# Attention and expert layer on one core: the turning of x moved ahead of the exponentials, logits by unit, first loads on two queues

## Chip, cores and metric

The kernel runs on one core of a Trainium2 chip. The metric is the time of one execution on the device in microseconds (us). Before the change it is 720.43 us, the median of three runs (719.71 to 723.58).

The core has a matrix engine (PE, with its weight loads PEld), a vector engine (DVE), an activation engine (ACT), a general engine (POOL) and a queue engine (SP) that here only issues transfers. ACT and POOL can issue transfers too. Matrix results go to eight PSUM banks of 128 x 512 numbers.

## What is computed

Sliding-window causal attention over 8 batches of 8 heads (576 positions, 64 numbers a head, a window of 64), then a layer with 8 experts, of which each token takes the one with the largest logit.

```python
scores = scale * q @ k.transpose(0, 1, 3, 2)
mask = (rel >= 0) & (rel < 64)
attn = softmax(where(mask, scores, -1e9))
x = (attn @ v).transpose(0, 2, 1, 3).reshape(4608, 512)

logits = x @ w_gate                      # 4608 x 8
e = argmax(logits, axis=1)
gate = softmax(logits)[row, e]
out[row] = gate[row] * (relu(x[row] @ w1[e]) @ w2[e])   # 512 -> 1024 -> 512
```

All is in float32.

## The kernel before, in words

The work has two stages. The first is an attention loop of 48 steps (up to about 220 us), the second runs the experts over tiles of 256 sorted tokens. The change touches the first stage and its seam with the second.

**Units and steps.** A *unit* is a pair of batches (`bg`, four of them) and a pair of heads (`g`, four). A unit has 1152 tokens, nine blocks of 128, and is done in three steps of three blocks, so there are 16 units and N = 48 steps. `step(s)` (line 941) works on several steps at once, as a pipeline written out by hand. Every engine runs its instructions in the order in which the program issues them. In one call of `step(s)` that order is:

- `scored(s + 1)` (628): PE, queries by keys into banks 0 and 1. `masked` (641): DVE adds the mask and takes the largest. `softened` (651): ACT, six exponentials.
- `weighted(s - 1)` (674): PE, values by turned probabilities into bank 6.
- `logit(s - 3)` (711): PE, the turned x of a step by the gate weights into bank 7.
- `flipped(s)` (659, 661): PE turns the probabilities, DVE copies the result of head 0 to `pT0`, ACT that of head 1 to `pT1`.
- `divided(s - 1)` (684 to 688): DVE divides by the sums of the exponentials and writes x to `xs`.
- loads for later units (every third step), all on SP: `load_rests`, `load_v`, `load_qk`. `load_v` also makes two copies of v on POOL.
- `turned(s + 3)` (595, 587): PE turns q and k, ACT copies. Steps 0 and 1 of a unit turn eight blocks, step 2 turns two.
- `x_turned(s - 2)` (699, 702): PE turns x, ACT copies it to `xT`.
- what stands in `todo[s]`: the routing of a finished pair of batches (`choose`, `place`, `weigh`, `store`), weight loads on ACT's queue, sums of weights on POOL.

Results of PE that ACT or DVE copies out go to banks 2 to 5 in turn (`tr_ring`): two from `flipped`, two or one from `turned`, one from `x_turned`.

**Ready logits.** In the last unit of a pair of batches `logit` returns true (`ripe`), and `by_tokens` copies that step's logits to `lgT`, turns them and writes them to `logits` by token. After the third such step `after` puts the routing into `todo`.

**The first table.** In the last routing inside the loop, `first_tiles` (902) runs in step 45: DVE makes a table of matches `hi_e`, PE multiplies it 54 times (914), DVE makes `perm_e` of the result, and POOL gathers the first tile of expert 0's tokens (`gather_first`, 280).

**Ahead of the loop** (920 to 928) SP issues 40 transfers: q and k of unit 0, gate weights, a zero row, the rests of the first pair (positions 512 to 575 of q, k, v), v of unit 0, q and k of unit 1, v of unit 1, q and k of unit 2. A transfer of q, k or v brings 128 KB in runs of 256 bytes.

**After the loop** (984 to 1044) the last `weighted`, the last logits and their routing run between parts of the first expert tile: `turn` turns the gathered tokens, `hidden` and `output` are its products, whose results use banks 0, 1, 6 and 4, 5, 7.

`any_number` (1092) is a branch for token counts that don't occur with these inputs.

Of the kernel before, what the change touches and what calls it, by code (L numbers as in the profile page):

```python
# [11 lines left out]
F32 = mybir.dt.float32  # L12
# [3 lines left out]
ALU = mybir.AluOpType  # L16
AX = mybir.AxisListType
# [19 lines left out]
def kernel(  # L37
# [458 lines left out]
    with tc.manual_schedule(), ExitStack() as held, ExitStack() as brief:  # L496
# [2 lines left out]
        rp = held.enter_context(tc.tile_pool(name="rp", bufs=2))  # L499
        att = brief.enter_context(tc.tile_pool(name="att", bufs=2))  # L500
        xp = brief.enter_context(tc.tile_pool(name="xp", bufs=3))
        sc_ring, tr_ring = cycle((0, 1)), cycle((2, 3, 4, 5))


# [32 lines left out]
        def load_qk(u):  # L537
            bg, g = units[u]
            qks[u] = [qk_m(((u % 3 + 2) % 3 * 2 + n) * 1024, BG, NV, 2, D) for n in range(2)]
            for i in range(BG):  # L540
                for t, src in zip(qks[u], (q, k)):
                    for h in range(2):
                        nc.sync.dma_start(
                            out=t[:, i, :, h, :],
                            in_=src[bg * BG + i, 2 * g + h, 0:SM, :].rearrange("(p j) d -> p j d", j=NV),
                        )

        def load_rests(bg):

            at = 6144 + bg % 2 * 2048  # L550
            vr = qk_m(at + 1024, BG, H, D)
            rests[bg] = [qk_m(at, H, D), qk_m(at + 512, H, D), vr]
            for t, src in zip(rests[bg], (q, k)):
                for i in range(BG):
                    nc.sync.dma_start(
                        out=t[i * D : (i + 1) * D], in_=src[bg * BG + i, :, SM:S, :].rearrange("h p d -> p h d")
                    )
            for i in range(BG):
                nc.sync.dma_start(out=vr[D:P, i], in_=v[bg * BG + i, :, SM:S, :].rearrange("h p d -> p h d"))
# [87 lines left out]
        def softened(prs, mx):  # L647
            for h in range(2):
                for m in range(ST):
                    y = prs[h][:, m, :]  # L650
                    nc.scalar.activation(out=y, in_=y, func=AF.Exp, scale=-1.0, bias=mx[:, h, m : m + 1])  # L651
            return prs
# [12 lines left out]
        def weighted(s, pTs):  # L665
            u, c = divmod(s, NST)
            bg, g = units[u]
            va, vb = v_ring[u % NVR]
            px = banks[6](0, 2, ST, VW)
            for m in range(ST):  # L670
                for a, (bp, i) in enumerate(blocks_of(c * ST + m)):
                    vt = va[:, bp, i // 2] if i % 2 or i == 0 else vb[:, bp, i // 2 - 1]
                    for h in range(2):
                        nc.tensor.matmul(  # L674
                            px[a * D : (a + 1) * D, h, m, :], lhsT=pTs[h][:, m, a * D : (a + 1) * D],
                            rhs=vt[:, h, :], start=True, stop=True, skip_group_check=True,
                        )
            return px
# [35 lines left out]
                )  # L714
            return g == NG - 1

        def by_tokens(bg, c):

            if c == 0:
                logits_of[bg] = rp.tile([P, NTB, E], F32, name="logits")  # L720
            lgT = rp.tile([ST * GE, P], F32, name="lgT")
            nc.scalar.copy(out=lgT[:], in_=lgs[bg][:, c, :])
            yield
            tr = banks[next(tr_ring)](0, ST, P)
            nc.tensor.transpose(out=tr[:, 0, 0 : ST * GE], in_=lgT[:], identity=ident[0 : ST * GE, 0 : ST * GE])
            V.tensor_copy(
                out=logits_of[bg][:, c * ST : (c + 1) * ST, :],
                in_=tr[:, 0, 0 : ST * GE].rearrange("p (m e) -> p m e", e=GE)[:, :, 0:E],
            )

        last = B // BG - 1
# [146 lines left out]
        def after(s, routing, bg):  # L878

            do = lambda n, op: todo.setdefault(s + n, []).append(op)  # L880
            part = lambda: next(routing, None)
            if bg < last - 1:
                for n in range(5):
                    do(n, part)

                for m in range(NTB):
                    do(5 + m * 2 // 3, partial(place, bg * NTB + m))
                    do(5 + m * 2 // 3, partial(weigh, bg, m, G))
                    if m % ST == ST - 1:
                        do(5 + m * 2 // 3, partial(store, bg, m // ST, G))  # L890
                return

            for n in (0, 0, 1, 2, 2):
                do(n, part)
            for m in range(NTB):
                do(3 + m // 3, partial(place, bg * NTB + m))
                do((2, 2, 3, 3, 4, 4, 4, 5, 5)[m], partial(weigh, bg, m, nc.scalar if m in (2, 6) else G))
                if m % ST == ST - 1:
                    do(3 + m // ST, partial(store, bg, m // ST, G))
            do(6, first_tiles)  # L900

        def first_tiles():

            V.scalar_tensor_tensor(
                out=key[:], in0=rkhi[:, 0:NJE], scalar=1.0, in1=oh_all[:, 0, 0:NJE], op0=ALU.add, op1=ALU.mult
            )
            V.tensor_tensor(
                out=hi_e[:], in0=_inner(key[:], NE * C), in1=_ins(hi_id[:, C + 1 : C + 1 + NE * C], 1, NJE),
                op=ALU.is_equal,
            )  # L910
            slots = banks[next(tr_ring)](0, NE * C)
            for j in range(NJE):
                for i in range(2):
                    nc.tensor.matmul(
                        slots, lhsT=lo[:, i, j], rhs=hi_e[:, j], start=(i + j == 0), stop=(i + j == NJE)
                    )
            V.tensor_scalar(out=perm_e[:], in0=slots, scalar1=-1.0, scalar2=float(NT), op0=ALU.mult, op1=ALU.add)
            gather_first(perm_e[:, 0:C])

        N = NU * NST  # L920
        load_qk(0)
        nc.sync.dma_start(out=wg[:, :, 0:E], in_=moe_w_gate.rearrange("(g p) e -> p g e", p=P))
        nc.sync.dma_start(out=x_dram[NT : NT + 1, :], in_=zrow[:])
        load_rests(0)
        load_v(0)
        load_qk(1)
        load_v(1)
        load_qk(2)

        for g in range(NG):  # L930
            step = NST * (g // 2) + g % 2 + 1
# [122 lines left out]
    with tc.manual_schedule():  # L1054
# [36 lines left out]

        def any_number():

            tiles_of = rt.tile([P, E, NTILE], F32, name="tiles_of")
            V.tensor_tensor(
                out=tiles_of[:], in0=_inner(cum[:], NTILE), in1=_ins(lane[:, 0:NTILE], 1, E), op=ALU.is_le
            )
            with nc.allow_low_precision("integers"):
                V.tensor_reduce(out=expert_i[:], in_=tiles_of[:].rearrange("p e t -> p t e"), axis=AX.X, op=ALU.add)
# [60 lines left out]
```

## Time and profile before

| what | us |
|---|---|
| median of three runs | 720.43 (719.71 to 723.58) |
| the profiled execution, its time | 726.15 |
| the profiled execution, its span (first to last instruction) | 724.4 |
| first `weighted` starts | 22.02 |
| `weighted` of step 2 to that of step 45 | 177.67 |
| `weighted` of step 45 to the last | 15.40 |
| from there to 240 us (first expert tile, last routing), PE busy throughout | 21.11 |
| mean granted PE clock over the span | 0.989 |

The span is what the trace shows; the time of the same execution is 1.75 us longer. In a line of the timeline the columns are start, busy time, engine, line of the program, operation, what is written and read, shape and count; in brackets stands how long the engine stood idle before and what ended that. PE's instructions overlap, so the busy time of a group is longer than the distance to the start of the next group. "PEclk" and the third column from the right in a table of stretches are the clock granted to PE, 1.00 being full speed. The DMA share can exceed 1, since transfers overlap within an engine.

### The profile page before, as it was taken

The page shows a single profiled execution, that of the slowest core. Times are in us where ns is not written, and L with a number is a line of the kernel's source. Part 1 is how long each engine was busy: PE and PEld are TensorE (multiplying, and loading weights), DVE is VectorE, ACT ScalarE, POOL GpSimd, SP SyncE. Part 2 cuts the span into 40 slices and gives each one's busy share as a digit, 9 for nine tenths or more (in the row PEclk, how much of TensorE's full clock was granted, in tenths as well). Part 3 has the DMA queues.
Part 4 walks back from the last instruction along what each step waited for, and adds up shares of the span by engine and source line. Part 5 has one row for each costly group of instructions (what it writes and reads, how often), then busy time and mean ns, then how long its engine had stood idle before and what let it go on. Part 6 is the DMA issues. An engine that isn't in the chain of part 4 may idle for free. (4 is left out here: it accounts for less than half of the span.)

```text
span 724.4 us, 17946 instructions
## 1 busy us (share of the span) xinstructions
PE 689.7 (95%) x6882; PEld 607.1 (84%) x6882; DVE 497.8 (69%) x1636; ACT 258.5 (36%) x653; POOL 350.7 (48%) x360
## 2 busy tenths in 40 slices
PE   5999999999879999999999999999999999999993
PEld 3887788888768898797999999899889799889993
DVE  3575898898965858675866686677766677666731
ACT  4787788888754211111211221112111111111110
POOL 4213748459375025937462356445274745272011
PEclk9999999999999999999999999999999999999997
DMA  8998898789361382715211531440261620111000
GB/s 159 219 195 186 176 188 230 168 188 235 106 194 47 121 291 81 258 59 202 102 38 60 161 133 57 154 170 30 88 243 59 242 69 30 61 37 61 2 30 28
DMA packets 137289, 93.37 MB, mean 129 GB/s; under 512 B 117009, under 2 KB 117009, under 8 KB 137171
## 3 DMA queue, kind: packets, MB, share of 16 engines
q1 hardware_dynamic: 127858, 62.16, 32.5%
q0 software_dynamic: 8736, 27.53, 11.7%
q10 hardware_dynamic: 576, 2.10, 0.9%
q8 instruction: 74, 1.21, 0.7%
q14 instruction: 45, 0.36, 0.2%
HBM read 72.89 MB, written 20.45 MB: 129 GB/s over the span
## 5 line engine op out<-in xcount | busy, mean ns | idle before, releaser
L315 DVE STREAM_TRANSPOSE v_m<-qk_m 32x256 f32<-32x256 f32 x304 | 132.4, 435 | 9.0 <-DMA qk_m<-x_dram,at_g 3.4
L344 PE MATMUL bank<-qk_m,s 128*128 128x128 f32 x1024 | 122.5, 275 | 1.0 <-DVE qk_m L365 1.0
L344 PEld LDWEIGHTS bank<-qk_m,s 128*128 128x128 f32 x1024 | 118.3, 192 | 1.2 <-issue 1.2
L275 POOL DMA_INDIRECT qk_m<-x_dram,at_g x38 | 41.0, 1080 | 142.4 <-DVE v_m L315 114.0
L651 ACT ACTIVATE pr<-pr,mx 128x128 f32<-128x128 f32 x288 | 89.7, 391 | 36.3 <-DVE mx L641 36.3
L344 PE MATMUL bank<-qk_m,w 128*128 128x128 f32 x768 | 93.8, 275 | 1.0 <-PEq L1077 0.9
L344 PEld LDWEIGHTS bank<-qk_m,w 128*128 128x128 f32 x768 | 90.6, 192 | 4.6 <-issue 4.2
L641 DVE CUSTOM_DVE_ANT_0 pr<-bank,mask 128x128 f32<-128x128 f32 x288 | 64.4, 286 | 30.7 <-PE bank L628 28.1
L295 POOL DMA_INDIRECT out_dram<-v_m,at_s x42 | 42.5, 1012 | 87.7 <-DVE v_m L384 85.1
L384 DVE TENSOR_TENSOR v_m<-bank,v_m 128x256 f32<-128x256 f32 (+1 forms) x95 | 43.8, 480 | 45.0 <-PE bank L388 30.1
L569 POOL COPY v_m<-v_m 64x520 f32<-64x520 f32 x32 | 19.8, 619 | 73.1 <-DMA v_m<-in_v_dram 72.5
L140 POOL TENSOR_TENSOR s<-w 128x1024 f32<-128x1024 f32 x22 | 52.2, 2372 | 0.0
L674 PEld LDWEIGHTS bank<-v_m,pT 128*64 128x64 f32 x1152 | 41.3, 141 | 12.0 <-DVE xs L688 5.8
L674 PE MATMUL bank<-v_m,pT 128*64 128x65 f32 x1152 | 47.9, 232 | 2.9 <-DVE xs L688 2.8
L388 PE MATMUL bank<-qkT_m,v_m 128*128 128x256 f32 x216 | 48.3, 379 | 0.0
L351 ACT COPY qk_m<-bank 128x512 f32<-128x512 f32 x16 | 9.4, 587 | 108.8 <-PE bank L344 63.2
L628 PE MATMUL bank<-qkT_m 64*64 64x128 f32 x1152 | 45.9, 290 | 0.1
L388 PEld LDWEIGHTS bank<-qkT_m,v_m 128*128 128x128 f32 x216 | 41.0, 190 | 5.5
L595 PE MATMUL bank<-ident,qk_m 128*128 128x128 f32 x256 | 37.0, 288 | 8.9 <-DMA qk_m<-in_q_dram 7.7
L444 PEld LDWEIGHTS bank<-qk_m,w 128*128 128x128 f32 x320 | 43.9, 190 | 0.9 <-issue 0.7
L444 PE MATMUL bank<-qk_m,w 128*128 128x160 f32 x320 | 44.4, 299 | 0.4 <-ACT qk_m L327 0.4
L659 PE MATMUL bank<-ident,pr 128*128 128x128 f32 x288 | 43.1, 287 | 0.0
(174 smaller groups left out, 1231.1 us busy)
## 6 DMA issues: line engine op xcount, KB each, us to landing
w<-in_moe_w_dram SPq DMA_DIRECT2D x11, 2048.0 KB, 10.0
qk_m<-in_q_dram SPq DMA_DIRECT2D x72, 128.0 KB, 3.8
qk_m<-in_k_dram SPq DMA_DIRECT2D x72, 128.0 KB, 3.7
v_m<-in_v_dram SPq DMA_DIRECT2D x64, 128.0 KB, 3.9
qk_m<-in_moe_w_dram SPq DMA_DIRECT2D x3, 2048.0 KB, 10.4
x_dram<-xs POOLq DMA_DIRECT2D x6, 512.0 KB
x_dram<-xs POOLq DMA_DIRECT2D x3, 768.0 KB
w<-in_moe_w_dram ACTq DMA_DIRECT2D x4, 512.0 KB, 4.3
```

The lines of the kernel that those rows point to most:

```text
L140: op()
L295: put = G.indirect_dma_start(out=out[:, :], out_offset=bass.IndirectOffsetOnAxis(ap=at_s[:, c : c + 1], axis=0), in_=ys[c], in_offset=None ...
L315: V.transpose(out=xn[b * QD : (b + 1) * QD, :, :, a * QD : (a + 1) * QD].rearrange("p c g i -> p (c g) i"), in_=rows[a * QD : (a + 1) * QD ...
L344: nc.tensor.matmul(acc[:, f, :], lhsT=a[:, g, f * P : (f + 1) * P], rhs=b[:, g, :], start=(first and f == 0 and g == 0), stop=(g == HG - 1 ...
L384: plus = lambda out, a, b: V.tensor_tensor(out=out, in0=a, in1=b, op=ALU.add)
L388: nc.tensor.matmul(acc, lhsT=a[:, f, :], rhs=b[:, f, :], start=(start and f == 0), stop=(stop and f == HF - 1), skip_group_check=True,)
L444: nc.tensor.matmul(acc[:, i], lhsT=w1[:, g, f * P : (f + 1) * P], rhs=xq[:, g].rearrange("p c s -> p (c s)")[:, 0:HALF], start=(i + g == 0 ...
L628: nc.tensor.matmul(out_, lhsT=qT[rows, t, a * WINDOW : (a + 1) * WINDOW], rhs=rhs, start=True, stop=True, skip_group_check=True,)
L641: V.tensor_tensor_reduce(out=prs[h][:, m, :], in0=scs[h][:, m, :], in1=mask[:, m0 + m, :], scale=-scale, scalar=-2 * MASKED, op0=ALU.add, ...
L651: nc.scalar.activation(out=y, in_=y, func=AF.Exp, scale=-1.0, bias=mx[:, h, m : m + 1])
L659: nc.tensor.transpose(out=tr[:, m, :], in_=prs[h][:, m, :], identity=ident[:])
L674: nc.tensor.matmul(px[a * D : (a + 1) * D, h, m, :], lhsT=pTs[h][:, m, a * D : (a + 1) * D], rhs=vt[:, h, :], start=True, stop=True, skip_ ...
```

## The change

- Ahead of the loop, the k transfers of unit 0 (four) and of the first rests (two) are issued on ACT's queue. The order becomes: q and k of unit 0, first rests, q and k of unit 1, v of units 0 and 1, gate weights, q and k of unit 2, the zero row.
- In `step(s)`, `x_turned(s - 2)` moves from behind `turned(s + 3)` to a place behind `logit` and ahead of the exponentials of step s + 1 and of `flipped(s)`. `masked` and `softened` are called separately for it.
- `logit` runs only in steps with s mod 3 = 2, then for three steps at once; `by_tokens` then copies, turns and writes all three at once, with a tile of its own pool.
- `first_tiles` is split: its DVE part stays in step 45, its products and the gather go to step 46.
- `weighted` of the last two steps writes to banks 0 and 1 in place of 6.
- `any_number` has its table in other memory.

```diff
@@ load_qk, load_rests
-                for t, src in zip(qks[u], (q, k)):
+                for t, src, queue in zip(qks[u], (q, k), (nc.sync, nc.sync if u else nc.scalar)):
                     for h in range(2):
-                        nc.sync.dma_start(
+                        queue.dma_start(
...
-            for t, src in zip(rests[bg], (q, k)):
+            for t, src, queue in zip(rests[bg], (q, k), (nc.sync, nc.sync if bg else nc.scalar)):
                 for i in range(BG):
-                    nc.sync.dma_start(
+                    queue.dma_start(
@@ weighted
-            px = banks[6](0, 2, ST, VW)
+            px = banks[6 if s < N - 2 else s - N + 2](0, 2, ST, VW)
@@ by_tokens
-        def by_tokens(bg, c):
+        def by_tokens(bg, c, n=1):
...
-            lgT = rp.tile([ST * GE, P], F32, name="lgT")
-            nc.scalar.copy(out=lgT[:], in_=lgs[bg][:, c, :])
+            lgT = (rp if n == 1 else lt).tile([ST * GE, n, P], F32, name=f"lgT{n}")
+            nc.scalar.copy(out=lgT[:], in_=lgs[bg][:, c : c + n, :])
             yield
-            tr = banks[next(tr_ring)](0, ST, P)
-            nc.tensor.transpose(out=tr[:, 0, 0 : ST * GE], in_=lgT[:], identity=ident[0 : ST * GE, 0 : ST * GE])
+            tr = banks[next(tr_ring)](0, n, ST * GE)
+            for i in range(n):
+                nc.tensor.transpose(out=tr[:, i], in_=lgT[:, i], identity=ident[0 : ST * GE, 0 : ST * GE])
...
@@ after
-            do(6, first_tiles)
+            table = first_tiles()
+            do(6, partial(next, table))
+            do(7, partial(next, table))
@@ first_tiles
                 op=ALU.is_equal,
             )
+            yield
             slots = banks[next(tr_ring)](0, NE * C)
...
             gather_first(perm_e[:, 0:C])
+            yield
@@ ahead of the loop
         load_qk(0)
+        load_rests(0)
+        load_qk(1)
+        load_v(0)
+        load_v(1)
         nc.sync.dma_start(out=wg[:, :, 0:E], in_=moe_w_gate.rearrange("(g p) e -> p g e", p=P))
+        load_qk(2)
         nc.sync.dma_start(out=x_dram[NT : NT + 1, :], in_=zrow[:])
-        load_rests(0)
-        load_v(0)
-        load_qk(1)
-        load_v(1)
-        load_qk(2)
@@ step
             if 0 <= s + 1 < N:
-                prs[s + 1] = softened(*masked(s + 1, scored(s + 1)))
+                prs[s + 1] = masked(s + 1, scored(s + 1))
             if 0 <= s - 1 < N:
                 px = weighted(s - 1, pTs.pop(s - 1))
-            ripe = 0 <= s - 3 < N and logit(s - 3)
+            ripe = 0 <= s - 3 < N and s % NST == NST - 1 and [logit(n) for n in range(s - 5, s - 2)][-1]
+            if 0 <= s - 2 < N:
+                x_turned(s - 2)
+            if 0 <= s + 1 < N:
+                prs[s + 1] = softened(*prs[s + 1])
             if 0 <= s < N:
                 pTs[s] = flipped(prs.pop(s))
...
             if s + 3 < N:
                 turned(s + 3)
-            if 0 <= s - 2 < N:
-                x_turned(s - 2)
             for op in todo.pop(s, ()):
                 op()
             if ripe:
-                bg, c = (s - 3) // (NG * NST), (s - 3) % NST
-                parts = by_tokens(bg, c)
+                bg = (s - 3) // (NG * NST)
+                parts = by_tokens(bg, 0, NST)
                 next(parts)
                 todo.setdefault(s + 1, []).append(partial(next, parts, None))
-                if c == NST - 1:
-                    after(s + 1, choose(bg), bg)
+                after(s + 1, choose(bg), bg)
```

More of the change, by code (lines that the diff above doesn't have):

```diff
@@ L501 @@
         xp = brief.enter_context(tc.tile_pool(name="xp", bufs=3))
+        lt = brief.enter_context(tc.tile_pool(name="lt", bufs=1))
         sc_ring, tr_ring = cycle((0, 1)), cycle((2, 3, 4, 5))
@@ L715, in logit @@
             return g == NG - 1
-        def by_tokens(bg, c):
+        def by_tokens(bg, c, n=1):
             if c == 0:
                 logits_of[bg] = rp.tile([P, NTB, E], F32, name="logits")
-            lgT = rp.tile([ST * GE, P], F32, name="lgT")
-            nc.scalar.copy(out=lgT[:], in_=lgs[bg][:, c, :])
+            lgT = (rp if n == 1 else lt).tile([ST * GE, n, P], F32, name=f"lgT{n}")
+            nc.scalar.copy(out=lgT[:], in_=lgs[bg][:, c : c + n, :])
             yield
-            tr = banks[next(tr_ring)](0, ST, P)
-            nc.tensor.transpose(out=tr[:, 0, 0 : ST * GE], in_=lgT[:], identity=ident[0 : ST * GE, 0 : ST * GE])
+            tr = banks[next(tr_ring)](0, n, ST * GE)
+            for i in range(n):
+                nc.tensor.transpose(out=tr[:, i], in_=lgT[:, i], identity=ident[0 : ST * GE, 0 : ST * GE])
             V.tensor_copy(
-                out=logits_of[bg][:, c * ST : (c + 1) * ST, :],
-                in_=tr[:, 0, 0 : ST * GE].rearrange("p (m e) -> p m e", e=GE)[:, :, 0:E],
+                out=logits_of[bg][:, c * ST : (c + n) * ST, :],
+                in_=tr.rearrange("p n me -> p (n me)").rearrange("p (m e) -> p m e", e=GE)[:, :, 0:E],
             )
@@ L1092, in any_number @@
         def any_number():
-            tiles_of = rt.tile([P, E, NTILE], F32, name="tiles_of")
+            tiles_of = v_m(2080, E, NTILE)
             V.tensor_tensor(
-                out=tiles_of[:], in0=_inner(cum[:], NTILE), in1=_ins(lane[:, 0:NTILE], 1, E), op=ALU.is_le
+                out=tiles_of, in0=_inner(cum[:], NTILE), in1=_ins(lane[:, 0:NTILE], 1, E), op=ALU.is_le
             )
             with nc.allow_low_precision("integers"):
-                V.tensor_reduce(out=expert_i[:], in_=tiles_of[:].rearrange("p e t -> p t e"), axis=AX.X, op=ALU.add)
+                V.tensor_reduce(out=expert_i[:], in_=tiles_of.rearrange("p e t -> p t e"), axis=AX.X, op=ALU.add)
             _, (tiles,) = nc.values_load_multi_w_load_instructions(
```

## The prediction

> **What bounds the kernel now.** I read the busy shares first, then busy time by stage, then the PE timeline of one step of the attention loop, then ACT's, then the waits. The chain that ended last is no help here: its answer holds the last 1 us only.
>
> ```profile
> PE 689.7 (95%) x6882; PEld 607.1 (84%) x6882; DVE 497.8 (69%) x1636; ACT 258.5 (36%) x653; POOL 350.7 (48%) x360
> ```
>
> PE is busy nearly always, but everything the change touches lies in the first 240 us, so the stages count.
>
> ```profile
> 25.82:203.49 177.67, 170.45 (x2977) 141.96 (x2973) 147.31 (x807) 146.48 (x431) 96.36 (x128) 0.99 0.83 192
> 203.49:218.89 15.40, 11.04 (x195) 9.05 (x196) 9.27 (x45) 6.67 (x20) 11.60 (x12) 0.89 0.46 149
> ```
>
> Columns: stretch, length, busy us of PE, weight loads, DVE, ACT, POOL, then clock, DMA share, GB/s. The first row runs from the second `weighted` (step 2) to that of step 45: 43 steps, 4.13 us each. PE is full, but ACT is at 146.48 of 177.67: there is little room before ACT's order matters.
>
> One step on PE (scored, weighted, logit, flipped, turned, x_turned, and the next scored):
>
> ```profile
> 156.47 0.89 PE L628 MATMUL bank<-qkT_m 64*64 64x128 f32 x24
> 157.29 0.97 PE L674 MATMUL bank<-v_m,pT 128*64 128x65 f32 x24
> 158.19 0.42 PE L711 MATMUL bank<-xT,wg 128*32 128x128 f32 x6
> 158.54 0.87 PE L659 MATMUL bank<-ident,pr 128*128 128x128 f32 x6
> 159.25 1.04 PE L595 MATMUL bank<-ident,qk_m 128*128 128x128 f32 x8
> 160.12 0.49 PE L699 MATMUL bank<-ident,xs 128*128 128x128 f32 x3
> 160.54 0.89 PE L628 MATMUL bank<-qkT_m 64*64 64x128 f32 x24
> ```
>
> Start to start: 0.82, 0.90, 0.35, 0.71, 0.87, 0.42, sum 4.07. In every third step `turned` has two blocks (0.22 at 163.32) and the step takes 3.42. Three steps of pure PE are 11.56, or 3.85 a step; 43 x 3.85 = 165.7, so 12.0 us of the 177.7 are stalls.
>
> The same step on ACT:
>
> ```profile
> 157.59 0.49 ACT L702 COPY xT<-bank 128x384 f32<-128x384 f32 x1
> 157.97 1.88 ACT L651 ACTIVATE pr<-pr,mx 128x128 f32<-128x128 f32 x6
> 159.73 0.47 ACT L661 COPY pT<-bank 128x384 f32<-128x384 f32 x1
> 160.09 1.08 ACT L600 COPY qkT_m<-bank 128x512 f32<-128x512 f32 x2
> 161.05 0.50 ACT L702 COPY xT<-bank 128x384 f32<-128x384 f32 x1
> ```
>
> ACT works in program order. From one start to the next: xT 0.38, six exponentials 1.76, pT 0.36, two turned copies 0.96. The pT copy (h = 1) stands behind the exponentials of the following step, and the next `weighted` needs it. Here it ended at 160.20 and `weighted` ran at 161.36: 1.16 us to spare, 0.3 in some two-block steps (ended 164.46, used 164.77).
>
> **Part 1, x_turned and its copy ahead of the exponentials: the term that decides.** Nothing is added or removed: three transposes and one copy a step. But the xT copy waits for `x_turned`, which now runs on PE after `weighted`; the six exponentials queue behind that copy on ACT, the pT copy behind them, and the next `weighted` waits for pT. That closes a loop from `weighted` to `weighted`. Its terms: weighted 0.90, x_turned start to xT start 0.64 from the place where ACT stood idle for it:
>
> ```profile
> 221.16 0.55 PE L699 MATMUL bank<-ident,xs 128*128 128x128 f32 x3
> 221.80 0.48 ACT L702 COPY xT<-bank 128x384 f32<-128x384 f32 x1 [0.24 <-PE bank L699]
> ```
>
> then xT 0.38, exponentials 1.76, pT 0.46, and 0.05 to PE (pT ended 184.75, the PE instruction that waited for it began 184.80). Sum 4.19, say 4.18. PE's own work in a four-block step without logits is 4.07 - 0.35 = 3.72, so PE would stand 0.46 before each `weighted`. DVE's masks don't set it: `scored` then starts 0.82 + 0.46 before `weighted`, the first mask 1.05 after that (156.47 to 157.52), some 2 us ahead of the exponentials. Behind pT on ACT stand the turned copies (0.96) and now and then another item (lgT, a weight DMA issue of 0.38, a weigh of 0.63): the next xT copy starts 0.51 + 0.90 + 0.64 = 2.05 after pT's start, and 0.36 + 0.96 + 0.63 fits, so these cost nothing; with less cover each would cost its own length.
>
> What it gives back: in the old order `x_turned` is the fifth claimant of a ring of four banks and waits for the same step's DVE pT copy:
>
> ```profile
> PEld bank L699 <- DVE pT L661: 5.0, 6, 2.0
> PE bank L699 <- DVE pT L661: 3.7, 4, 1.8
> ```
>
> That wait goes. It lies within the 12.0 us of stalls, which a loop at 4.18 can mostly swallow.
>
> **Part 2, logits by unit.** Eighteen matmuls in every third step in place of six in each. PE's sum is the same (weighted to flips took 0.90 before any logit ran, so a logit costs 0.35 and no more). But all three lie in the loop of part 1, between `weighted` and `x_turned`: 3 x 0.35 = 1.05 more in that step. Fourteen such steps (5, 8 .. 44). Nine separate lgT copies (0.20 each) become three of one 96x384 copy, and nine transposes and copies to logits go in three lots, in PE and ACT time that is now idle: 0.
>
> Loop: 43 x 4.18 + 14 x 1.05 = 194.4 against 177.7: **+16.8**. Bounds: with 4.10 and 1.0 it is 190.3 (+12.6); with 4.25 it is 197.5 (+19.8).
>
> **DVE in the longer loop.** A step needs 6 x 0.21 + 0.47 + 0.90 = 2.6 us of it, so 1.5 are left, and some 2.2 may come at once: `divided` ends 3.4 after `weighted`, and masks, pT copy and `divided` (2.7) must start by 4.18 + 1.43 to free bank 6 for the one after. Batch 2's routing puts 2.8 in one step (189.05 to 191.83), its place calls 1.3 to 2.4 a step. **+1**, bounds 0 and 4.
>
> **Part 3, two first queues and the new order of loads.** SP issues 40 DMAs ahead of the loop at 0.66 each (two in 1.33). Six go to ACT's queue. An ACT issue of this shape isn't shown; a weight issue there took 0.33 to 0.38, SP's 0.66: 2 to 4 us, done by 0.8 + 1.28 (table load) + 4.0 = 6.1 against the first ACT copy at 5.83. I take 0.66; the 0.3 is hidden because PE has 16 cold transposes (0.27 each, 4.71 to 9.1) before it uses a copy. SP then reaches q and k of unit 1 at 0.8 + 8 x 0.66 = 6.1 instead of 13.77, v of unit 0 at 11.4 as before.
>
> ```profile
> 13.77 1.24 SPq L543 DMA_DIRECT2D qk_m<-in_q_dram  x2
> 18.31 2.29 PE L595 MATMUL bank<-ident,qk_m 128*128 128x128 f32 x8 [1.63 <-DMA qk_m<-in_q_dram]
> 22.02 1.37 PE L674 MATMUL bank<-v_m,pT 128*64 128x65 f32 x24
> ```
>
> The wait at 18.31 goes; what is late next is v of unit 0 with POOL's copies, ready at 17.2. Wholly cold, PE comes to the first `weighted` at 9.1 + scored 1.5, masks to 12.1, scored 1.5, flips 1.5, turned 2.2, scored 1.5 = 18.8. So it starts 3.2 to 4.8 earlier; nothing if the DMA engines (0.57 of the time in the first 10 us, 1.14 in the next) can't go faster. **-4**, bounds 0 and -4.8. wg and the zero row, two issues, move behind loads and are used no sooner than step 5. The later stall at 54 to 60 us (q of unit 4) is in the 12.0; all SP loads stand 4 us earlier and PE comes there at 21.8 + 7 x 4.18 + 2 x 1.05 + 2.0 = 55.2 instead of 54.2, so it goes.
>
> **Part 4, the end of the loop.** The first table's DVE part stays in step 45, its 54 matmuls (1.43) and gathers go to 46, where pT makes PE wait anyway; `weighted` of the last two uses banks 0 and 1, so it no longer waits for `divided` (0.77 and 0.88). Before: 15.40 from step 45's `weighted` to the last. After: 4.18 + 4.18 + (0.90 + 1.05 + 0.42 + 0.95 from flips to the pT copy (216.81 to 217.76) + 0.48 + 0.05) = 12.2: **-3.2**, bounds -2 and -4. POOL's two gathers, each behind a 0.54 memset, now start some 5 us before `turn` reads them and land 3.5 after their issue; before, the first one started 2.3 after its table. **+0.5**, bounds 0 and 2.3. The other-number branch doesn't run.
>
> Sum: 16.8 + 1 - 4 - 3.2 + 0.5 = **+11.1**. On the profiled execution: span 724.4 to 735.5, its own time 726.15 to 737.3. The median of the runs is 720.43, so **731.5**.
>
> **A rule that speaks against it.** PE's new gaps of 0.5 to 1.1 us are shorter than the 1.75 at 88.23, after which the clock stayed full (24 scored matmuls in 0.89), while the two gaps around 56 us were followed by a clock of 0.50 (1.56). So I take the full clock. The Trainium skill, "TensorE: Matmul & The Clock Gate", under "A second HAM failure mode: psum-queue depth-cycling", says that small repeated idles between groups of matmuls can alone make the clock swing; by it the sum would be that of the third rival.
>
> **Rivals.** *Faster, 705:* the loop of part 1 doesn't bind. For it: ACT waits 22.2 us for DVE's masks between 30 and 175 us, room for the copy, and the bank ring's wait goes. PE alone gives 165.7 + 3 of DVE stalls - 177.7 = -9; with -4, -3.2, +0.5: -15.7. It needs pT 0.46 earlier in plain steps and 1.1 in logit steps; ACT's program order stands against it. 11 in 100. *No change, 722:* the head's early start is the larger part: the loop at its low bound (+12.6), head and end at their best (-4.8, -4), DVE 0 make +3.8, 724; with one more of the old stalls (2 us) gone, 722. 10 in 100. *Clock lost, 760:* weighted, transposes and scored at cold prices (+0.45 and +0.3 in the loop): 43 x 0.75 = 32 more. 7 in 100. The forecast has 72.
>
> **Numbers.** A measurement tells 0.5% (3.6 us) from no change. The main case spans 725 to 739: half of the summed bounds on each side, since they won't all fall on one. Down to 721 most of the draw is in, and 2 in 10 are left out. Range 721 to 739. Faster 0.11, same 0.10, slower 0.79.
>
> **What would show it.** Right: `weighted` to `weighted` 4.2 and 5.2 us, PE waiting at L674 for ACT's pT by 29 x 0.46 + 14 x 1.1 = 29 us in all, ACT waiting at L702 for PE, the first `weighted` near 18. Wrong: steps of 3.7, or L702 starting without a wait; a head no earlier than 21; clock under 0.9 in the loop.

## The result, and the profile after

| | before | after |
|---|---|---|
| median of four runs, us | 722.0 (719.71 to 726.19) | 733.38 (730.95 to 735.34) |
| ratio | 1 | 1.015, 95% interval 1.0114 to 1.0185 |
| profiled execution: its time / its span | 726.15 / 724.4 | 734.07 / 732.4 |
| start to `weighted` of step 2 | 25.82 | 26.85 |
| step 2 to step 45 | 177.67 | 187.30 |
| step 45 to the last `weighted` | 15.40 | 12.41 |
| all that follows | 505.5 | 505.8 |

The kernel became slower by 1.5%. The forecast was 731.5 on 720.43, a ratio of 1.0154. By stages the forecast was less good than its sum: the loop grew by 9.6 us (17.8 forecast, DVE's 1 among them), the head by 1.0 (4.0 less forecast), the end shrank by 3.0 (3.2 forecast). The two misses partly cancel, to 8.0 us in the spans of the two traces where 11.1 were forecast. The medians differ by 11.4, since the profiled execution of before was one of the slower of its runs (4.2 us above their median, the one of after 0.7).

The busy shares of the changed kernel:

```profile
PE 692.9 (95%) x6882; PEld 613.2 (84%) x6882; DVE 491.9 (67%) x1630; ACT 258.3 (35%) x647; POOL 350.1 (48%) x360
```

They say nothing of the change: the same matmuls, six small DVE and six ACT instructions fewer (the nine lgT copies and the nine copies to logits, now three and three). The stages do, with the columns of the table of stretches as before:

```profile
26.85:214.15 187.30, 175.11 (x2977) 148.58 (x2973) 141.43 (x801) 146.11 (x425) 95.26 (x126) 1.00 0.77 181
214.15:226.56 12.41, 10.18 (x195) 8.60 (x195) 8.72 (x43) 6.45 (x20) 8.09 (x10) 1.00 0.44 143
```

In the loop ACT does the same 146 us of work as before in 9.6 us more, at a full clock. So nothing costs more; something waits more. What waits is in the waits (engine and line, what it waited for, us in total, times, longest):

```profile
ACT xT L703 <- PE bank L700: 46.8, 45, 2.5
...
PE bank L675 <- ACT pT L662: 6.3, 15, 0.4
...
PEld bank L675 <- ACT pT L662: 13.2, 37, 0.6
```

Before, ACT stood 36.3 us for DVE's masks, work of the step to come. Now it stands 46.8 us for `x_turned`, and PE's weight loads stand 13.2 us for ACT's pT (the 6.3 us of the matmuls lie inside these waits, so they don't add up). Each waits for the other once in most steps, which is what a closed chain looks like. The timeline of one plain step of the changed kernel shows it (start, busy, engine):

```profile
113.03 0.46 ACT L662 COPY pT<-bank 128x384 f32<-128x384 f32 x1
113.12 1.33 PE L675 MATMUL bank<-v_m,pT 128*64 128x65 f32 x24
113.39 1.07 ACT L601 COPY qkT_m<-bank 128x512 f32<-128x512 f32 x2
114.39 0.55 PE L700 MATMUL bank<-ident,xs 128*128 128x128 f32 x3
114.97 0.48 ACT L703 COPY xT<-bank 128x384 f32<-128x384 f32 x1 [0.52 <-PE bank L700]
115.35 1.86 ACT L652 ACTIVATE pr<-pr,mx 128x128 f32<-128x128 f32 x6
116.39 0.89 PE L629 MATMUL bank<-qkT_m 64*64 64x128 f32 x24
117.11 0.46 ACT L662 COPY pT<-bank 128x384 f32<-128x384 f32 x1
```

Follow the starts: pT 113.03, `weighted` (which stretches from 0.97 to 1.33: its first matmul, 2 of the 24 records, uses head 0 and goes ahead, the rest stands until this pT is there), x_turned 114.39, xT 114.97, exponentials 115.35, pT 117.11. That is 1.36 + 0.58 + 0.38 + 1.76 = 4.08 us, and three such steps with one lot of logits take 4.53 + 4.42 + 4.09 = 13.04. Before, the same three took 4.07 + 4.07 + 3.42 = 11.56, the sum of PE's own work.

### The profile page after: what moved, and what is told of

Read it like the earlier page. It is cut to its first block, busy times and chain, and to the rows that moved or that the text cites. A ratio compares the mean times of both kernels' runs of the same rounds, so it can differ in the third digit from the quotient of the medians.

```text
span 732.4 us, 17932 instructions
## 1 busy us (share of the span) xinstructions
PE 692.9 (95%) x6882; PEld 613.2 (84%) x6882; DVE 491.9 (67%) x1630; ACT 258.3 (35%) x647; POOL 350.1 (48%) x360
## 3 DMA queue, kind: packets, MB, share of 16 engines
q8 instruction: 74, 1.21, 0.7%
## 5 line engine op out<-in xcount | busy, mean ns | idle before, releaser
L675 PE MATMUL bank<-v_m,pT 128*64 128x65 f32 x1152 | 59.4, 229 | 16.0 <-ACT pT L662 6.3
L675 PEld LDWEIGHTS bank<-v_m,pT 128*64 128x64 f32 x1152 | 47.0, 139 | 31.3 <-ACT pT L662 13.2
L662 DVE COPY pT<-bank 128x384 f32<-128x384 f32 x48 | 26.7, 557 | 42.2 <-PE bank L660 42.0
L596 PE MATMUL bank<-ident,qk_m 128*128 128x128 f32 x256 | 36.3, 287 | 7.5 <-DMA qk_m<-in_q_dram 6.9
## 6 DMA issues: line engine op xcount, KB each, us to landing
qk_m<-in_moe_w_dram SPq DMA_DIRECT2D x3, 2048.0 KB, 11.1
```

What stands on the lines that cost most here:

```text
L675: nc.tensor.matmul(px[a * D : (a + 1) * D, h, m, :], lhsT=pTs[h][:, m, a * D : (a + 1) * D], rhs=vt[:, h, :], start=True, stop=True, skip_ ...
```

## Experiments

Diffs are against the changed kernel, unless they say otherwise. Every ratio is to the kernel before, run beside it on the same chip, with its 95% interval; "loop" is step 2 to step 45 in the experiment's trace, "end" step 45 to the last `weighted`. The changed kernel has 1.015, 187.30 and 12.41.

### x_turned back in its old place

```diff
@@ step
-            if 0 <= s - 2 < N:
-                x_turned(s - 2)
             if 0 <= s + 1 < N:
                 prs[s + 1] = softened(*prs[s + 1])
...
                 turned(s + 3)
+            if 0 <= s - 2 < N:
+                x_turned(s - 2)
```

> Part 1 undone alone: x_turned and its copy stand behind turned again, all else as after the change. Theory (the chain weighted, x_turned, xT copy, six exponentials, pT copy, weighted sets the pace): the stretch from step 2's weighted to step 45's falls from 187.3 us to 176 to 179, as before the change, and the total by 8 to 11 us, to 722 to 725. Rival (the slower pace comes from the logits in one lot and from DVE, not from the place of x): the stretch stays above 185 us and the total above 731.

Measured: 721.18 us, ratio 0.9964 (0.9934 to 0.9993), loop 173.23, end 11.11. Plain steps take 3.72, 3.72 and 3.85. So with part 1 undone and parts 2 to 4 kept, the loss is gone, and 14.1 us of the loop with it. The loop is even shorter than expected (176 to 179); the logits in one lot, which are kept, save 0.27 in every three steps (below), 3.8 us in all. It doesn't yet say why: the move changes the place of the transposes on PE, of the copy on ACT and the order of the banks all at once.

### The exponentials behind the turned probabilities

Here x stays ahead, as in the change. Only the exponentials of step s + 1 go behind the pT copy of step s, so that ACT's order is xT, pT, exponentials.

```diff
@@ step
                 x_turned(s - 2)
-            if 0 <= s + 1 < N:
-                prs[s + 1] = softened(*prs[s + 1])
             if 0 <= s < N:
                 pTs[s] = flipped(prs.pop(s))
+            if 0 <= s + 1 < N:
+                prs[s + 1] = softened(*prs[s + 1])
```

> x_turned stays ahead, but the six exponentials move behind flipped, so that on ACT the pT copy comes before them. Theory: the chain is cut, PE alone sets the pace (11.6 us for three steps); the stretch of 43 steps falls from 187.3 to 167 to 172 us and the total to 713 to 719, faster than both kernels. Rival (ACT's wait for x_turned as such holds the loop, whatever stands behind it): the stretch stays above 183 us, the total above 729.

Measured: 718.71 us, 0.9939 (0.9909 to 0.9969), loop 171.09, end 11.33. The timeline of a step of this kernel:

```profile
114.34 0.48 ACT L703 COPY xT<-bank 128x384 f32<-128x384 f32 x1
115.00 0.48 ACT L662 COPY pT<-bank 128x384 f32<-128x384 f32 x1 [0.18 <-PE bank L660]
115.38 1.86 ACT L652 ACTIVATE pr<-pr,mx 128x128 f32<-128x128 f32 x6
115.77 0.89 PE L629 MATMUL bank<-qkT_m 64*64 64x128 f32 x24
116.58 0.97 PE L675 MATMUL bank<-v_m,pT 128*64 128x65 f32 x24
```

pT now ends at 115.48, 1.1 us before `weighted` needs it, and `weighted` is back at 0.97. This is the decisive run: x is as early as in the changed kernel, the one thing taken out is the 1.76 us of exponentials between xT and pT, and 16.2 us of the loop go. Loop and time both came as expected. What is left of a loss is in every third step, 4.10 in place of 3.85: there `weighted` waits for `divided` to free bank 6 (PE's weight loads stood 10.9 us for L689, in 25 waits).

### Part 1 alone

The diff of the first experiment in reverse, on the kernel before.

```diff
@@ step (before)
-                prs[s + 1] = softened(*masked(s + 1, scored(s + 1)))
+                prs[s + 1] = masked(s + 1, scored(s + 1))
...
+            if 0 <= s - 2 < N:
+                x_turned(s - 2)
+            if 0 <= s + 1 < N:
+                prs[s + 1] = softened(*prs[s + 1])
...
-            if 0 <= s - 2 < N:
-                x_turned(s - 2)
```

> The kernel before with part 1 alone: x_turned and its copy ahead of the exponentials, a logit in every step. Theory: 43 steps of 4.08 + 0.35, 190 to 193 us in place of 177.7, head and end as before, the total 12 to 16 us above the kernel before, 734 to 738. Rival (part 1 costs only together with the logits in one lot): the stretch stays within 180 us, the total within 725.

Measured: 743.04 us, 1.0289 (1.0254 to 1.0323), loop 192.21, end 17.87. The loop came as expected, the time 5 us above what was. The first part by itself costs twice what the whole change does; the other parts give half of it back. In its end PE waits 2.93 us for the table, and the 24 scored matmuls behind it take 1.56. But the kernel before had nearly that wait too (2.71), so this isn't why the end is longer than its 15.40: all three steps are, 8.47, 5.21 and 4.19 against 7.50, 4.57 and 3.33.

### One logit in each step

```diff
@@ step
-            ripe = 0 <= s - 3 < N and s % NST == NST - 1 and [logit(n) for n in range(s - 5, s - 2)][-1]
+            ripe = 0 <= s - 3 < N and logit(s - 3) and s % NST == NST - 1
```

> Part 2 undone on PE alone: one logit in every step again, by_tokens still by unit. Theory (a logit lies inside the chain wherever it stands before x_turned): 43 x 0.28 to 0.35 in place of 14 x 0.80, the stretch goes from 187.3 to 188 to 191 us, the total to 734 to 737. Rival (logits are PE work that fits into PE's waits): the stretch falls by 5 us or more, the total to 728 or less.

Measured: 738.61 us (734 to 737 were expected), 1.0214 (1.0172 to 1.0255), loop 190.44. Three steps take 4.77 + 4.44 + 4.09 = 13.30, against 13.04. So inside the chain the logits cost either way, and one lot of three is cheaper by 0.26: 18 matmuls run in 0.79 us (118.47 to 119.26 in the changed kernel) where three lots of six took 3 x 0.35. Where no chain binds, the lot saves as much: 3.72 + 3.72 + 3.85 = 11.29 with x_turned in its old place, against 11.56 before. So by the loops of the traces part 2 is a gain of about 3 us (by the times the two intervals just touch), not the 14.7 us loss that the forecast had for it against a chain with no logits at all: those logits had to be paid in the chain in any case.

### The head: four orders of the first loads

Three kernels, all with the chain in place: both parts undone (`head_old`: all on SP in the old order), the new order on SP alone (`one_queue`), the old order with k and the k rests on ACT's queue (`two_q_old_order`).

```diff
@@ load_qk, load_rests: head_old and one_queue
-                for t, src, queue in zip(qks[u], (q, k), (nc.sync, nc.sync if u else nc.scalar)):
+                for t, src, queue in zip(qks[u], (q, k), (nc.sync, nc.sync)):
@@ ahead of the loop: head_old and two_q_old_order
         load_qk(0)
+        nc.sync.dma_start(out=wg[:, :, 0:E], in_=moe_w_gate.rearrange("(g p) e -> p g e", p=P))
+        nc.sync.dma_start(out=x_dram[NT : NT + 1, :], in_=zrow[:])
         load_rests(0)
-        load_qk(1)
         load_v(0)
+        load_qk(1)
         load_v(1)
...
```

> Part 3 undone alone: all loads on SP in the old order. Theory, from the trace of after: the head gained nothing, the weighted of step 2 starts at about 26 us as in both kernels, the total is 731 to 734. Rival, as the prediction had it: the early loads are worth 4 us, the weighted of step 2 comes later than 29 us, the total is 736 to 738.

> The kernel after with its new order of loads, but all of them on SP. Theory (the DMA engines are full from the first loads on, so a second queue moves no data sooner; v of unit 0 now stands behind q and k of unit 1): v of unit 0 is issued at about 15.3 us as with two queues, the weighted of step 2 starts at 24 to 28 us, the total is 732 to 735. Rival, as the prediction had it (the second queue saves SP's issue time): the weighted of step 2 comes 4 us later than with two queues, after 29 us, the total is 737.

> The kernel after with the old order of loads, but the k loads of unit 0 and the rests on ACT's queue. Theory (the order is what spoiled the head, since v of unit 0 came late): v of unit 0 is issued before 12 us, PE has no long wait in the first weighted, the weighted of step 2 starts at 22 to 25 us, the total is 729 to 732. Rival (the second queue itself spoils the head, through the late table load and slower first loads): 26 us or later, 733 or more.

| | ratio | v of unit 0 issued at | `weighted` of step 2 |
|---|---|---|---|
| the change | 1.015 (1.0114 to 1.0185) | 15.30 | 26.85 |
| head_old | 1.0145 (1.0101 to 1.0188) | 11.46 | 26.07 |
| one_queue | 1.0174 (1.0141 to 1.0206) | 15.70 | 26.91 |
| two_q_old_order | 1.0131 (1.0098 to 1.0165) | 10.35 | 24.04 |

All four intervals overlap: against the kernel before, no part of part 3 makes a difference that these ratios can tell. Two of the kernels can be compared more closely, since they ran on the same chip: the four runs of `two_q_old_order` (731.02 to 733.46) all lie below the four of `one_queue` (734.73 to 735.67). With four runs each that is a hint, no more, that the old order on two queues is some 2 to 3 us better than the new order on one. The starts of step 2 all came where they were expected, the times within 0.6 us of it. The traces say why the hoped-for start didn't come. The queues of the changed kernel:

```profile
0.81 2.98 ACTq L544 DMA_DIRECT2D qk_m<-in_k_dram  x4
4.35 2.61 ACTq L556 DMA_DIRECT2D qk_m<-in_k_dram  x2
6.99 1.28 ACT L601 ACT_TABLE_LOAD   x1 [6.99 <-DMA qk_m<-in_k_dram]
9.22 1.24 SPq L544 DMA_DIRECT2D qk_m<-in_q_dram  x2
15.30 6.03 SPq L567 DMA_DIRECT2D v_m<-in_v_dram  x8
...
15.82 0.46 ACT L662 COPY pT<-bank 128x384 f32<-128x384 f32 x1
...
19.25 0.30 PE L675 MATMUL bank<-v_m,pT 128*64 128x65 f32 x2 [1.54 <-DVE mx L642]
...
21.06 1.19 PE L675 MATMUL bank<-v_m,pT 128*64 128x65 f32 x16 [0.80 <-POOL v_m L574]
```

and the same place in `one_queue`:

```profile
15.70 5.41 SPq L567 DMA_DIRECT2D v_m<-in_v_dram  x8
...
20.31 0.30 PE L675 MATMUL bank<-v_m,pT 128*64 128x65 f32 x2 [2.67 <-DMA v_m<-in_v_dram]
```

Both kernels issue the same 22 transfers ahead of v. On two queues that took until 15.30, on one until 15.70: the second queue issued six of them and bought 0.4 us. From 5 to 14 us the table of stretches gives the changed kernel a DMA share of 1.37 at 182 GB/s, `one_queue` 0.99 at 190: busier, with no more data. And v of unit 0 now stands behind q and k of unit 1. The first `weighted` has its last pT at 16.28, but it starts at 19.25, after PE stood 1.54 us, and its rest waits for POOL's copies of v until 21.06. The profile puts the 1.54 down to DVE's masks, which this `weighted` doesn't read; in `one_queue` the same wait (2.67) is put down to the transfer of v.

The Trainium skill, "DMA: Bandwidth & Descriptors", under "Issuing engines are not separate DMA queues", states that transfers started by different engines run on the same 16 DMA engines, so that issuing from several saves only the time of issuing. In these two traces the data did move no faster (182 GB/s against 190); of the time of issuing, 0.4 us of 14.9 were saved. Whether the issues slowed down because the DMA engines were full was not tried.

How much a single trace says of the head is limited. Six of the kernels here, the changed one among them, issue these same first loads (the experiments on the loop, the table and the banks leave them alone), and in them `weighted` of step 2 starts between 23.57 and 27.65 (in the four that also keep the change's order of a step, between 23.57 and 27.04). The scored matmuls show what differs, first in the changed kernel, then in the one with a logit in each step:

```profile
10.33 0.89 PE L629 MATMUL bank<-qkT_m 64*64 64x128 f32 x24
...
25.36 1.56 PE L629 MATMUL bank<-qkT_m 64*64 64x128 f32 x24
```

```profile
10.28 1.56 PE L629 MATMUL bank<-qkT_m 64*64 64x128 f32 x24
...
22.75 0.89 PE L629 MATMUL bank<-qkT_m 64*64 64x128 f32 x24
```

By these times one has the fast clock at 10 us and loses it from 22 to 27, the other is slow at 10 and fast after 18. The granted clock of the table of stretches shows the loss (0.50 from 22 to 26), but it has 1.00 at 10 us in both, so for the first 17 us the times alone speak. So some 3 us of the head can be a matter of which execution was traced, nearly as much as the forecast's whole term.

### The end: the table in one step, the last values in bank 6

```diff
@@ one_step_table
-            do(7, partial(next, table))
+            do(6, partial(next, table))
@@ px_bank6
-            px = banks[6 if s < N - 2 else s - N + 2](0, 2, ST, VW)
+            px = banks[6](0, 2, ST, VW)
```

> The kernel after with the first table in one step, 45, as before; banks and all else as after. Theory (the split takes PE's wait for DVE's hi_e out of the end): PE waits about 2 us for hi_e, the end from step 45's weighted to the last grows from 12.4 to 14 to 15.5 us, turn no longer waits 0.7 us for the gather, the total goes up by 1 to 2.5 us. Rival (the end is set by the pT chain, which covers the table anyway): 12.4 to 13 us, the total the same or 0.7 us less.

> The kernel after with the last two weighted in bank 6 again. Theory: in the new order the last weighted waits for pT on ACT and for flips, and divided of the step before is done by then, so the banks are worth 0 to 0.5 us: the end stays at 12.4 to 12.9, the total the same. Rival, as the prediction had it (each of the two waits 0.8 us for divided): 13.5 to 14, the total 1 to 1.6 us more.

Measured: the table in one step gives 735.26 us, 1.0192 (1.0144 to 1.024), and an end of 16.86, more than expected (14 to 15.5), so the split is worth 4.4 us there, in the trace; by the times the interval overlaps that of the change. Its timeline, and the same place in the kernel before:

```profile
216.21 1.60 PE L919 MATMUL bank<-hi_e,lo 128*128 128x4 bf16 x54 [3.19 <-DVE hi_e L911]
217.74 1.56 PE L629 MATMUL bank<-qkT_m 64*64 64x128 f32 x24
```

```profile
208.64 1.49 PE L914 MATMUL bank<-hi_e,lo 128*128 128x4 bf16 x54 [2.71 <-DVE hi_e L907]
```

PE waits 3.19 us for the table (2.71 before), and the 24 scored matmuls behind the wait take 1.56 in place of 0.89. In the changed kernel the 54 matmuls run a step later and wait for nothing:

```profile
221.20 1.50 PE L919 MATMUL bank<-hi_e,lo 128*128 128x4 bf16 x54
```

Bank 6 for the last values gives 735.07 us, 1.0164 (1.0118 to 1.021), and an end of 13.32, between what was expected and its rival: the last `weighted` waits 1.21 us for `divided`, so the two banks are worth 0.9 in the trace; in the times it is no difference.

### A version that beats both

`best_v_first` takes what helped: exponentials behind pT, `divided` ahead of `flipped` (so that bank 6 comes free sooner), v of unit 0 ahead of q and k of unit 1, all on SP; logits by unit and the end as in the change.

```diff
@@ ahead of the loop (and the queue lines as in one_queue)
-        load_qk(1)
         load_v(0)
+        load_qk(1)
@@ step
-            if 0 <= s + 1 < N:
-                prs[s + 1] = softened(*prs[s + 1])
-            if 0 <= s < N:
-                pTs[s] = flipped(prs.pop(s))
             if 0 <= s - 1 < N:
                 divided(s - 1, px)
+            if 0 <= s < N:
+                pTs[s] = flipped(prs.pop(s))
+            if 0 <= s + 1 < N:
+                prs[s + 1] = softened(*prs[s + 1])
```

> The kernel after with the exponentials behind flipped, divided ahead of flipped on DVE, all loads on SP and v of unit 0 ahead of q and k of unit 1. Theory: with the chain cut, a third step's 4.10 us came from weighted waiting for divided to free bank 6, so now three steps take 3.72 + 3.72 + 3.85; the stretch of 43 steps is 163 to 168 us, the end 11.3, the weighted of step 2 at 23 to 26, the total 712 to 716. Rival (the third step's wait is DVE's whole load, not its order): three steps stay at 11.5 or more, the total at 717 to 720.

Measured: 717.96 us, 0.994 (0.9917 to 0.9963); the step-2 `weighted` starts at 23.51, the loop takes 173.93. Undisturbed steps are at 3.72, 3.72, 3.85, and the third step's extra quarter of the version with the exponentials behind pT is gone, as expected. The loop and the time are not (163 to 168 and 712 to 716 were expected). The loop is even 2.8 longer than in that version, whose head ended 3 us later. Of the 12 us that it lacks to 43 such steps, 7 lie in four long ones early on (6.06, 4.83, 6.31 and 4.62). In the longest of them PE is early for its loads:

```profile
55.66 0.63 PE L596 MATMUL bank<-ident,qk_m 128*128 128x128 f32 x4 [0.67 <-DMA qk_m<-in_q_dram]
57.21 0.63 PE L596 MATMUL bank<-ident,qk_m 128*128 128x128 f32 x4 [0.93 <-DMA qk_m<-in_k_dram]
57.77 1.49 PE L629 MATMUL bank<-qkT_m 64*64 64x128 f32 x24
```

Two waits of under 1 us, and the scored matmuls behind them at 1.49: a step of 6.31. It is level with the second experiment (718.71), and both are 0.6% faster than the kernel before.

### Weight loads out of the way of the first 60 us

The first expert's weights are loaded in steps 1 to 5 of the loop, in the same stretch. Two versions of the last kernel load them later, with the sums that POOL forms of them later too.

```diff
@@ ahead of the loop: best_w1_later (best_w1_mid: 3 for 6, and 16 + n for 8 * NST + n)
-            step = NST * (g // 2) + g % 2 + 1
+            step = NST * (g // 2 + 6) + g % 2 + 1
...
-            todo.setdefault(3 * NST + n, []).append(op)
+            todo.setdefault(8 * NST + n, []).append(op)
```

> best_v_first with the first expert's w1 (four transfers of 512 KB) loaded in steps 19 to 23 in place of 1 to 5, and its sums on POOL in steps 24 to 27 in place of 9 to 12. Theory (with the chain cut the loads of the first 60 us set the pace, DMA share near 1 there): the long steps 4 to 11 (6.06, 4.83, 6.31, 4.62) shrink to under 4.3 each, the stretch of 43 steps goes from 173.9 to 165 to 169 us, the total to 710 to 714. Rival (the transfers of q, k and v alone, at SP's pace of issue, hold these steps): they stay above 5 us, the total at 716 to 719.

> best_v_first with w1 of the first expert loaded in steps 10 to 14 and its sums in steps 16 to 19, ahead of the first weigh and store on POOL. Theory (best_w1_later freed steps 4 to 23 of every wait but put the sums between weigh and store on POOL, so that divided waited for stores in steps 28 to 33): no step from 2 to 36 above 5 us, the stretch of 43 steps 163 to 169 us, the total 708 to 714. Rival (the transfers are only late elsewhere, in the stretch from 60 to 110 us): steps 13 to 24 show waits of 6 us or more in all, the total at 715 to 719.

Measured: 723.54 us, 1.0015 (0.9991 to 1.004), loop 176.53, and 722.45 us, 1.0004 (0.9981 to 1.0026), loop 174.28. Both lose what `best_v_first` had gained, and both miss what was expected (710 to 714 and 708 to 714). The early stalls do go: in the first of the two, the steps from 3 to 15 all take 3.72, 3.72, 3.85. But the sums now run while POOL is needed for the routing. With the loads in steps 19 to 23, the rows of x are stored late, and DVE waits before it may write xs:

```profile
126.14 0.56 DVE L689 TENSOR_TENSOR xs<-bank,rec 128x384 f32<-128x384 f32 x1 [3.95 <-DMA x_dram<-xs]
```

That step took 8.71. With the loads in steps 10 to 14 the sums meet DVE's marks of places, in bf16:

```profile
100.17 0.31 DVE L804 TENSOR_SCALAR lo<-lane,low,tok_a 128x128 bf16<-128x128 bf16 x1
...
103.33 2.36 POOL L972 TENSOR_TENSOR s<-w 128x1024 f32<-128x1024 f32 x1
104.43 1.32 DVE L804 TENSOR_SCALAR lo<-lane,low,tok_a 128x128 bf16<-128x128 bf16 x1
105.65 2.36 POOL L972 TENSOR_TENSOR s<-w,s 128x1024 f32<-128x1024 f32 x1
105.67 2.40 DVE L804 TENSOR_SCALAR lo<-lane,low,tok_b 128x128 bf16<-128x128 bf16 x1
```

In both, the work that follows the loads is what had no room. The new place of the loads in steps 10 to 14 may not be free either: there PE stands 1.72 us at 75.8 ahead of turning q and k, and what ended that wait the profile doesn't show for certain.

## Why the prediction was right, and where not

- **The chain of part 1: right, a little long.** The steps named (weighted, x_turned, xT, six exponentials, pT) are the ones in the trace, in that order, and cutting one link of it (the second experiment) opens it. The sum was 4.18; it measured 4.08. The excess lies in two terms: pT's start to x_turned's, 0.46 + 0.05 + 0.90 = 1.41 in the forecast, measured 1.36 (2 of the 24 records of `weighted` run before pT), and x_turned to xT, 0.64 in the forecast, measured 0.58. The 0.10 over 43 steps is 4.3 us of the loop's excess of 8.2.
- **Logits in the chain: the right place, too high a price.** The term was 3 x 0.35 = 1.05 in a step; 18 matmuls in a row cost 0.80 (pT to pT 4.88 in such a step). Over 14 steps that is 3.5 us. That price was taken from groups of six; why 18 in a row cost less than three groups isn't shown.
- **The signs that were named.** ACT stands for PE at xT, as named. From `weighted` to `weighted` it is 4.53, 4.42 and 4.09, where 4.2 and 5.2 were named, since `weighted` begins with head 0's matmul; from pT to pT it is 4.08 and 4.88. PE's loads wait 13.2 us for pT in place of 29. Another 9.5 us in 19 waits are put down to `divided`, which frees bank 6 for the same `weighted`; where both occur, as at 121.75 and 122.50, pT comes last. The first `weighted` starts at 19.25, near the 18 that was named, but without its v.
- **DVE in the longer loop:** 1 was taken. The loop has 187.30 against 43 x 4.08 + 14 x 0.80 = 186.6, so 0.7 remain for everything else; that they are DVE's wasn't separated.
- **The head: wrong, in size and sign.** The step that failed is that SP reaches q and k of unit 1 at 6.1 and "v of unit 0 at 11.4 as before". It priced the two queues as if each kept 0.66 an issue on its own. In the trace SP's issues of the first pair's rests took 2.54 for two while ACT issued too, q and k of unit 1 came at 9.22 and v of unit 0 at 15.30. The six transfers moved to ACT were thus no start on the rest, and v had been put behind four pairs of loads. The bounds, 0 to -4.8, left out the case that the order itself makes v late; +1.0 came, of which the clock of this one execution may be 3 either way. `two_q_old_order` against `one_queue` points to the order of v as the loss, but the two also differ in their queues, and the times alone don't settle it. A small slip besides: the 16 cold transposes of before ended at 9.77, not at 9.1.
- **The table load behind ACT's issues: the right place, 2.2 us too early.** It was to be done, with the issues, by 6.1; the load ran from 6.99 to 8.27, the first copy at 8.28 where 5.83 was before. The six issues took 6.2 us in place of 4.0. PE stood 0.30 for a copy at 10.33.
- **The end: right in sum.** -3.2 forecast, -3.0 measured, and the two experiments give 4.4 for the split and 0.9 for the banks. They add to more than 3.0, since with the chain in place each step of the end is longer: 17.87 (x_only) less 5.3 is 12.5. By steps it was 5.07, 3.42 and 3.93, where 4.18, 4.18 and 3.85 were forecast; in the first of them PE stood 0.79 for DVE's masks, so the near hit holds some luck. The gather had +0.5; PE waited 0.71 for it:

```profile
229.08 0.66 PE L306 MATMUL bank<-ident,qk_m 128*128 128x128 f32 x4 [0.71 <-DMA qk_m<-x_dram,perm_e]
```

- **The full clock in the loop: right.** PE's loads stand up to 0.6 us for pT in most steps, its matmuls up to 0.48, for 187 us, and the granted clock of the stretch is 1.00, so the third rival (760; its own sum gives 763) fell. What the rule of repeated small idles would have made of it isn't seen here. Nor do these runs give a length from which an idle costs the clock. It was at 0.50 after 2.93 us (end of part 1 alone), after 3.19 (table in one step) and after 0.67 and 0.93 close together (56 us in `best_v_first`). But `best_v_first` kept 1.00 after 2.12 us at 29.4, and waits of 0.79, 0.20 and 0.48 at 216 to 219 left it at 1.00 in the changed kernel, while the same three in `head_old` were followed by 0.50.
- **The other rivals.** That the chain doesn't bind (705) is excluded by the first two experiments. Its number was wrong besides: with the chain open the loop took 171.09, where it had 168.7, and the head gave nothing. No change (722) needed the head at its best.

- **The range.** It was said to be half of the summed bounds on each side; by the bounds as given that is 728 to 738, a little narrower than the 725 to 739 of the main case. The measured time fits either.

So the mechanism was right, and the closeness of the sum is in part luck, twice over. The loop's excess of 8 us was met by a head that was 5 us too good, which leaves the forecast 3.1 us above the 8.0 of the traces. That the medians show 11.4, and so meet 11.1, comes from the traced execution of before, which was 4.2 us slower than its median.

## What to carry to other kernels

When an instruction is moved on an engine that runs in order, write down the loop it closes: who waits for it, what is queued behind it there, and who waits for that; the sum of the starts round that loop is a floor for the step, whatever the busy shares say. If the loop binds, don't move the whole thing back before asking which one link can go behind: here six exponentials moved by one place turned 1.5% slower into 0.6% faster. And price a second DMA queue from a trace with two queues, and an order of loads by the first reader of each.

## What the runs showed that was not expected

- **DVE's bf16 marks stop while POOL works.** 0.31 us alone; 1.32 and 2.40 beside POOL's 2.36-us sums, and both end 0.06 after a sum ends (105.75 against 105.69, 108.07 against 108.01). The Trainium skill, "SBUF — State Buffer", under "SBUF: two separate sides", states that a fast DVE mode and POOL share a pair of ports which the first takes for its whole instruction while the other is blocked. The two ends agree with that: DVE is let go when the sum is done. That these marks run in the fast mode which is meant isn't shown.
- **Two DMA queues made the engines busier, not faster:** 1.37 of share for 182 GB/s, against 0.99 for 190 (5 to 14 us, one trace each).
- **A lot of like matmuls costs less than its parts:** 0.79 for 18, 3 x 0.35 for three times six, in the chain and out of it.
- **The clock of the first 27 us varies between executions of the same head** by enough to move the second `weighted` by 3.5 us (23.57 to 27.04 in four kernels that differ only behind it), so that a head must be compared by the times of many runs, not by one trace each.
